# A third of VectorE's exponential shifts, and the attention products with the reciprocal sums, moved to GpSimd; a reordered instruction plan

## The chip, the cores and the metric

The kernel runs on one core of a Trainium2 chip. The core has five engines that run their own instruction streams and meet only at semaphores: TensorE (matrix products, writes PSUM), VectorE and ScalarE (elementwise work, read PSUM and SBUF), GpSimd (elementwise work on SBUF alone) and SyncE, which here issues nearly all DMAs. In the profile they are PE (weight loads apart as PEld), DVE, ACT, POOL and SP. The metric is the device time of one execution in microseconds (us).

## The reference

Two independent blocks on 2048 rows of 512 columns, in bfloat16, written side by side.

```python
# A: 32 query heads of 16, one shared key/value head
q = (x @ wq) -> 32 heads; k = x @ wk; v = x @ wv
p = softmax(q k^T / 4);  a = concat(p v) @ wo
# B: linear attention, 32 heads of 16
pq, pk = q w_phi, k w_phi                  # per head, 16 x 16
phi = concat(softmax(p), softmax(-p))      # 32 features
o = phi_q (phi_k^T v) / (phi_q . sum(phi_k) + 1e-6);  b = o @ wo
out = concat(a, b, axis=-1)
```

Block A needs 32 x 2048 x 2048 exponentials. They are nearly all of the elementwise work.

## The kernel before, in words

**Tiles of block A.** The 2048 x 2048 scores of 32 heads are cut into 32 *accumulations* (`sc`, each with four heads at 512 queries, 16 key blocks of 128). One accumulation has 16 quads, a quad has four score tiles of 128 keys x 512 queries, one per head, 2048 tiles in all. A score tile is one matmul with 32 rows (`score`, L1611); four tiles sit on the four row groups of TensorE. The weighted sums of a quad are added into one PSUM bank (`ACC`) by matmuls with 32 output columns, again four side by side.

**Two ways to an exponential.** Each quad goes one of two ways.

- ScalarE: `expo` (L1672) reads three or two tiles from PSUM banks 0 to 2 or 3 to 4, and writes exp into the ring `PT` (20 tiles). `pv` (L1726) sums a quad with four matmuls.
- VectorE: `next_dq` takes one free bank per tile. `bits` (L1782) turns scores into the bit pattern of an fp16 power of two, as int16: one multiplication and one addition, PSUM to SBUF, `Z[:, 0]`. Then three `shift`s (L1795) add 256, 512 and 768 to all four tiles' 2048 integers, a quarter of an octave each, into `Z[:, 1]` to `Z[:, 3]`. `d_pv` (L1828) sums the four versions, with values weighted by four constants `K`, in 16 matmuls: a weighted mean of four coarse exponentials. There are three such buffers (`NQ`).

In the last accumulation both ways also sum the denominators into a second bank.

**After an accumulation.** `finish_sc` copies the bank to `accS` (L1426) and gathers the row of sums by four DMAs; `finish_sc2` takes the reciprocal of it (L1860) and spreads it by eight more DMAs into `denS`; `finish_sc3` multiplies `accS` by `denS` (L1878, all 31 on VectorE) into `On`. `outproj` (L1897) and `outproj2` project and store it, in 12 blocks. The last accumulation is finished by `out_part` (L1917) and `finish_last`.

**Block B** (`jobs_b`) runs in between: its projections on TensorE, its exponentials on ScalarE (L2050, L2140), its sums, reciprocals and scalings on VectorE.

**What sets the order.** Python code writes out the whole order before the kernel is built. `plan` makes jobs, each with an engine, an assumed duration, its predecessors and a priority; `run` simulates the engines and repeatedly issues the job that can start first, the lower priority number first among those within 0.02 us of it (`rank`). `dq_ok` lets the next VectorE tile start while VectorE's outstanding work (`dbusy`) is at most 3 us. So how many quads go to VectorE is an outcome of the planned times. On the chip each engine runs its stream in that order, with semaphores for the data. Where the plan leaves TensorE idle or lightly used it adds dummy matmuls with zero weights (`put_fill`, `fill` L1420; `company` L1403). The planner's DMA latencies are constants in the calls of `dmas`.

GpSimd has only setup work in the first 22 us, and one small job of block B (`b_kvfin`, L2118).

Of the kernel before, what the change touches and what calls it, by code (L numbers as in the profile page):

```python
# [1169 lines left out]
class _Fast:  # L1170
# [16 lines left out]
    def __init__(self, nc, st, ins, out):  # L1187
# [33 lines left out]
        self.ones = sb("ones", [128, 128], BF)  # L1221
        self.zero = sb("zero", [128, 128], BF)
# [40 lines left out]
        self.last_full = 0.0  # L1263

# [16 lines left out]
    def dmas(self, fs, reads, writes, us, is_output=False):  # L1281

        if self.rec is not None:
            return
        self.S.batch_begin("sp", is_output)
        for f in fs:
            self.S.dma(f, reads=reads, writes=writes)
        self.S.batch_end()
        for r in reads:
            self.tr[r] = max(self.tr.get(r, (0.0, "sp")), (self.fin + us, "sp"))  # L1290
        for w in writes:
            self.tw[w] = (self.fin + us, "sp")
# [37 lines left out]
    def issue(self, j, start):  # L1330
# [11 lines left out]
        self.te[j.eng] = max(self.te[j.eng], start + dur)  # L1342
        self.fin = start + dur + self.TAIL[j.eng]
# [90 lines left out]
    def head(self):  # L1434
# [47 lines left out]
        add("pool", lambda g: g.memset(self.bmx, 0.0), writes=["bmx"])  # L1482
        mask = self.mask
# [15 lines left out]
        for k, t in (("wk_rep", 4.5), ("half1", 3.0), ("wv", 5.5), (("wq", 0), 5.0), (("wq", 1), 16.0), (("VA1", 0), 5.0), (("VA1", 1), 12.0), ("odd", 14.0), ("ones", 1.0), ("zero", 1.0), ("bmx", 8.0)):  # L1499
            self.tw[k] = (t, "sp")  # L1500
# [10 lines left out]
    def jobs_a(self):  # L1511
        ps, xT, job = self.ps, self.xT, self.job
        for kc in range(4):
# [5 lines left out]
            job(("aK", kc), "dve", 0.60, (lambda kc: (lambda: self.absmax(self.KR[:, 0, kc * 512:kc * 512 + 512], kc, [("KR", 0, kc)])))(kc), after=[("KR", 0, kc)], prio=6, rel=30.0 + 5 * kc)  # L1519
# [3 lines left out]
        for ch in range(16):  # L1523
# [4 lines left out]
            job(("aq", ch), "dve", 0.60, (lambda ch: (lambda: self.absmax(self.QA[:, ch % 3, :], 4 + ch, [("QA", ch % 3)])))(ch), after=[("qa", ch)], prio=6, rel=0.0 if ch else 30.0)  # L1528
# [3 lines left out]
        for i in range(4):  # L1532
            job(("pp", i), "pe", 0.87, (lambda i: (lambda: self.out_part(i)))(i), mode="full", nb=1, prio=2.0, ok=lambda: self.ended,
                after=[("on", 24 + a) for a in range(7)])
        for sc in range(31):
            job(("rc", sc), "dve", 0.16, (lambda sc: (lambda: self.finish_sc2(sc)))(sc), after=[("ac", sc)], prio=1.1)
            job(("on", sc), "dve", 0.60, (lambda sc: (lambda: self.finish_sc3(sc)))(sc), prio=1.3,
# [20 lines left out]
    def absmax(self, src, col, reads):  # L1558
        self.add("dve", lambda v: v.tensor_reduce(out=self.mq[:, col:col + 1], in_=src, axis=AX.X, op=ALU.max, apply_absolute_value=True),
                 reads=reads, writes=[("mq", col)])  # L1560
# [107 lines left out]
    def expo(self, n0, us, b0):  # L1668
# [5 lines left out]
        if self.rec is None:  # L1674
# [3 lines left out]
            for n in range(n0, n0 + size):  # L1678
                if n % 4 == 3:
                    q = n // 4  # L1680
                    self.job(("pv", q), "pe", 0.44 if self.aquads[q][0] == 31 else 0.22, (lambda q: (lambda: self.pv(q)))(q), mode="col", prio=1.5,
                             after=[("vb" if self.aquads[q][0] % 2 else "va", self.aquads[q][1] // 4)] + ([("pv", q - 1)] if q else []),
                             ok=(lambda sc: (lambda: self.acc_ok(sc)))(self.aquads[q][0]))
# [29 lines left out]
    def pv(self, q):  # L1713
# [8 lines left out]
        for bank, w, (start, stop) in todo:  # L1722
# [22 lines left out]
    def next_dq(self):  # L1745
# [33 lines left out]
        def bits():  # L1779
# [4 lines left out]
            if self.rec is None:  # L1784
                self.dz_out -= 1
                self.dbusy += 1.2 if h == 3 else -0.6
# [6 lines left out]
        def shift(t):  # L1793
            def go():
                self.add("dve", lambda v: v.tensor_scalar(out=Z[:, t], in0=Z[:, 0], scalar1=256.0 * t, scalar2=None, op0=ALU.add),  # L1795
                         reads=zk, writes=[("Zt", p, t)])
                if self.rec is None:
                    self.dbusy -= 0.6
            return go
        for t in range(1, 4):  # L1800
            self.job(("dS", quad, t), "dve", 0.60, shift(t), after=[("dz", k - x) for x in range(4)], prio=2)
        aft = [("dS", quad, t) for t in range(1, 4)]
# [5 lines left out]
    def d_pv(self, quad):  # L1808
# [7 lines left out]
        rd += [("Z", p, h) for h in range(4)] + [("Zt", p, t) for t in range(1, 4)]  # L1816
# [17 lines left out]
    def d_pd(self, quad):  # L1834
# [4 lines left out]
        rd = ["onesK"] + [("Z", p, h) for h in range(4)] + [("Zt", p, t) for t in range(1, 4)]  # L1839
        self.d_sums(self.den_bank, self.onesK, self.Z[:, p].bitcast(F16), sl, start, stop, rd)  # L1840

    def finish_sc(self, sc):
# [10 lines left out]
        self.dmas(fs, [("accS", r)], [("denC", r)], 4.4)  # L1853
# [3 lines left out]
    def finish_sc2(self, sc):  # L1857
# [8 lines left out]
        self.dmas(fs, [("denR", r)], [("row", r), ("denS", r)], 4.4)  # L1866
# [5 lines left out]
        self.dmas(fs, [("row", r)], [("denS", r)], 11.0)  # L1872

    def finish_sc3(self, sc):
# [3 lines left out]
        self.add("dve", lambda v: v.tensor_tensor(out=o, in0=accS[:, r, :], in1=R[:, r, :], op=ALU.mult),  # L1878
                 reads=[("accS", r), ("denS", r), ("row", r)], writes=[key])
        if r:  # L1880
# [4 lines left out]
            self.dmas(fs, [key], [("On", sl)], 5.0)  # L1885
# [15 lines left out]
    def outproj2(self, qt):  # L1901
# [5 lines left out]
        self.dmas([lambda q: q.dma_start(dst, oa[:, ring, :])], [("outA", ring)], [], 4.0, is_output=True)  # L1907


    def out_part(self, i):  # L1910
        ps, On = self.ps, self.On
        bank = self.bank(("pp", i))

        def fn(pe):
            mm = None
            for A in range(4):
                mm = pe.matmul(ps[:, bank, :], lhsT=On[:, A, i * 128:i * 128 + 128], rhs=self.wo2[:, A, :], start=(A == 0), stop=False)  # L1917
            return mm
        self.add("pe", fn, reads=[("On", A) for A in range(4)] + ["wo2"], writes=[("PS", bank)])

    def finish_last(self):
# [8 lines left out]
        for h in range(2):  # L1930
# [3 lines left out]
            for i in range(2 * h, 2 * h + 2):  # L1934
                bank = self.bank(("pp", i))
# [494 lines left out]
```

## Time and profile before

| | us |
|---|---|
| median of 3 runs | 769.65 (767.93 to 771.23) |
| the profiled execution's own time | 767.89 |
| its span, first to last instruction | 765.8 |
| PE / DVE / ACT / POOL busy | 716.3 / 712.0 / 742.8 / 18.5 |

TensorE's granted clock was 0.995 on average. *Busy* is the union of an engine's instructions; a group's *mean* is one instruction from start to end, and neighbours on VectorE overlap by some 0.08 us. *Idle before* tells how long the engine had stood still before the instructions of the group, and the line after the arrow what ended that. A DMA queue's row is an issue, with the time to landing.

### The profile page before, as it was taken

What the parts mean: (1) busy time and instruction counts of PE and PEld (TensorE: products, weight loads), DVE (VectorE), ACT (ScalarE), POOL (GpSimd) and SP (SyncE); (2) the same over time, 40 slices, a digit from 0 to 9 for tenths busy, and PEclk for the clock granted to TensorE, in tenths of its full rate; (3) what the DMA queues carried; (4) which work ended last, traced back from release to release, by engine and by line L of the source; (5) the groups of instructions that cost most, each with busy time, mean ns of one, the idle gap of its engine ahead of it and who ended that gap; (6) DMA issues with size and microseconds to landing.
All of it is one profiled execution on the core that took longest, in us unless ns stands there. A gap on an engine that the chain in (4) does not pass through costs nothing.

```text
span 765.8 us, 17760 instructions
## 1 busy us (share of the span) xinstructions
PE 716.3 (94%) x7536; PEld 240.5 (31%) x7596; DVE 712.0 (93%) x1242; ACT 742.8 (97%) x694; POOL 18.5 (2%) x73
## 2 busy tenths in 40 slices
PE   7999999999998999999999999999999999999997
PEld 3332333233332333333332332223333333333222
DVE  3999999999998998799999999999997999999991
ACT  5999999999999999999999999999998999999996
POOL 6000000000000002000000000000000000000000
PEclk9999999999999999999999999999998999999999
DMA  9911011111012101110111110112111011111102
GB/s 183 206 9 8 6 8 13 8 10 12 1 12 36 9 6 8 13 9 16 19 9 19 16 15 14 15 11 30 22 20 8 20 28 25 23 15 12 10 8 38
DMA packets 47521, 18.15 MB, mean 24 GB/s; under 512 B 38468, under 2 KB 45572, under 8 KB 47432
## 3 DMA queue, kind: packets, MB, share of 16 engines
q1 hardware_dynamic: 44920, 16.47, 16.6%
q8 instruction: 61, 1.00, 0.5%
q10 hardware_dynamic: 2512, 0.44, 0.4%
q14 instruction: 28, 0.23, 0.1%
HBM read 2.15 MB, written 4.19 MB: 8 GB/s over the span
## 4 chain that ended last, share of the span: by engine, by line
ACT 73%; DVE 12%; PE 11%; DMA 2%; SPq 1%; issue 0%; ACTq 0%
ACT f_PT L1672 70%; DVE f_Z L1782 4%; PE f_ps L1611 3%; DVE f_Z L1795 3%; PE f_ps L1828 2%; ACT f_ET L2140 2%; PE f_ps L1726 2%; ACT f_Ek L2050 1%; DVE f_ssum L2056 1%; DMA f_AxT<-in_A_x_dram 1%; DVE f_vS L2082 1%; DVE f_Wk L2196 1%; PE f_ps L1420 1%; PE f_ps L1403 0%; PE f_ps L1917 0%
## 5 line engine op out<-in xcount | busy, mean ns | idle before, releaser
L1672 ACT ACTIVATE f_PT<-f_ps 128x1536 bf16<-128x1536 f32 x623 | 716.3, 1311 | 14.9 <-DVE f_VK L1581 8.2
L1782 DVE TENSOR_SCALAR f_Z<-f_ps 128x512 int16<-128x512 f32 x492 | 320.7, 680 | 17.4 <-PE f_ps L1611 15.8
L1611 PE MATMUL f_ps<-f_QA,f_KR 32*128 32x512 bf16 x2048 | 314.7, 385 | 23.2 <-ACT f_PT L1672 11.2
L1795 DVE TENSOR_SCALAR f_Z<-f_Z 128x2048 int16<-128x2048 int16 x369 | 243.0, 684 | 0.4
L1611 PEld LDWEIGHTS f_ps<-f_QA,f_KR 32*128 32x128 bf16 x2048 | 81.7, 91 | 237.7 <-ACT f_PT L1672 134.5
L1726 PE MATMUL f_ps<-f_PT,f_VA 128*32 128x512 bf16 x1556 | 153.5, 391 | 2.2 <-DVE f_accS L1426 1.8
L1828 PE MATMUL f_ps<-f_Z,f_VK 128*32 128x512 f16 x1968 | 129.5, 383 | 1.1 <-DVE f_accS L1426 0.4
L1726 PEld LDWEIGHTS f_ps<-f_PT,f_VA 128*32 128x32 bf16 x1556 | 38.7, 93 | 98.9 <-issue 88.3
L1420 PE MATMUL f_ps<-f_ones,f_zero 128*128 128x512 bf16 (+10 forms) x372 | 66.2, 345 | 3.0 <-POOL f_zero L1438 1.3
L1828 PEld LDWEIGHTS f_ps<-f_Z,f_VK 128*32 128x32 bf16 x1968 | 42.4, 96 | 56.9 <-issue 12.6
L1403 PE MATMUL f_ps<-f_ones,f_zero 32*128 32x512 bf16 x144 | 49.4, 380 | 0.3
L1420 PEld LDWEIGHTS f_ps<-f_ones,f_zero 128*32 128x32 bf16 (+2 forms) x372 | 19.1, 97 | 32.7 <-issue 21.9
L2196 DVE TENSOR_TENSOR f_Wk<-f_ps,f_wq 128x512 bf16<-128x512 f32 x32 | 21.8, 683 | 0.0
L1426 DVE COPY f_accS<-f_ps 128x512 f32<-128x512 f32 x31 | 21.3, 686 | 0.1
L2140 ACT ACTIVATE f_ET<-f_ps 128x512 bf16<-128x512 f32 x32 | 20.1, 772 | 0.0
L2082 DVE TENSOR_TENSOR f_vS<-f_ps,f_rs 128x1024 bf16<-128x1024 f32 x16 | 19.5, 1219 | 0.0
L2056 DVE TENSOR_REDUCE f_ssum<-f_Ek 128x64 f32<-128x1024 bf16 x16 | 19.3, 1208 | 0.1
L2050 ACT ACTIVATE f_Ek<-f_ps 128x512 bf16<-128x512 f32 x32 | 19.3, 721 | 0.0
L2072 PE MATMUL f_ps<-f_Bwv,f_BxT 128*128 128x512 bf16 x53 | 14.3, 380 | 2.8 <-DVE f_outA L1426 1.2
L2133 PE MATMUL f_ps<-f_BxT,f_Wq 128*128 128x512 bf16 x54 | 14.5, 380 | 2.0 <-issue 1.2
L2042 PE MATMUL f_ps<-f_Wk,f_BxT 128*128 128x512 bf16 x57 | 15.0, 381 | 1.4 <-issue 0.6
L1403 PEld LDWEIGHTS f_ps<-f_ones,f_zero 32*128 32x128 bf16 x144 | 11.4, 92 | 15.1 <-issue 11.4
(100 smaller groups left out, 320.6 us busy)
## 6 DMA issues: line engine op xcount, KB each, us to landing
f_denS<-f_denS SPq DMA_DIRECT2D x124, 30.0 KB, 3.1
out_dram<-f_outB SPq DMA_DIRECT2D x16, 128.0 KB, 2.7
f_denC<-f_accS SPq DMA_DIRECT2D x124, 2.0 KB, 1.7
f_denS<-f_denC SPq DMA_DIRECT2D x124, 2.0 KB, 1.7
out_dram<-f_outA SPq DMA_DIRECT2D x14, 128.0 KB, 2.1
f_On<-f_Od SPq DMA_DIRECT2D x60, 16.0 KB, 1.8
f_Bwv<-in_B_wqkv_dram SPq DMA_DIRECT2D x1, 512.0 KB, 4.7
f_Bwo<-in_B_wo_dram SPq DMA_DIRECT2D x1, 512.0 KB, 5.3
```

Of the source, the lines that this page charges most:

```text
L1403: self.add("pe", lambda pe: pe.matmul(out, lhsT=zero[0:32, :], rhs=rhs, start=False, stop=False, tile_position=(0, 0)), reads=["ones", "ze ...
L1420: mm = pe.matmul(ps[x:x + m, bank, 0:n].rearrange("p (a n) -> p a n", n=128), lhsT=zero[0:r, 0:m], rhs=rhs, start=start, stop=start, **kw)
L1611: return pe.matmul(self.ps[:, bank, :], lhsT=self.KR[32 * g:32 * g + 32, sc % 2, kap * 128:(kap + 1) * 128], rhs=self.QA[32 * g:32 * g + 3 ...
L1672: self.add("act", lambda a: a.activation(out=PT[:, sl[0]:sl[0] + size, :], in_=ps[:, b0:b0 + size, :], func=ACT.Exp), reads=[("PS", b0 + i ...
L1726: mm = pe.matmul(ps[32 * g:32 * g + 32, bank, :], lhsT=w, rhs=PT[:, slots[g], :], start=start, stop=stop, tile_position=(0, 32 * g))
L1782: self.add("dve", lambda v: v.tensor_scalar(out=o, in0=ps[:, bank, :], scalar1=self.Z1, scalar2=self.Z0, op0=ALU.mult, op1=ALU.add), reads ...
L1795: self.add("dve", lambda v: v.tensor_scalar(out=Z[:, t], in0=Z[:, 0], scalar1=256.0 * t, scalar2=None, op0=ALU.add), reads=zk, writes=[("Z ...
L1828: mm = pe.matmul(ps[32 * g:32 * g + 32, bank, :], lhsT=w[:, k, :], rhs=Zf[:, k, sl[g], :], start=start and k == 0, stop=stop and k == 3, t ...
L2050: self.add("act", (lambda a, sg: (lambda e: e.activation(out=Ek[:, r, a].rearrange("p h f -> p (h f)"), in_=ps[:, bank, :], func=ACT.Exp, ...
L2082: self.add("dve", lambda v: v.tensor_tensor(out=vS[:, :, :, 0:16], in0=v3, in1=rs.unsqueeze(3).to_broadcast([128, 2, 32, 16]), op=ALU.mult ...
L2140: self.add("act", lambda e: e.activation(out=self.ET[:, sl, :], in_=self.ps[:, bank, :], func=ACT.Exp, scale=sg), reads=[("PS", bank)], wr ...
L2196: self.add("dve", lambda v: v.tensor_tensor(out=o, in0=i, in1=w.unsqueeze(3).to_broadcast([128, 16, 2, 16]), op=ALU.mult), reads=[("PS", b ...
```

## The change

1. `shift` takes an engine. VectorE makes the versions 1 and 2 as before. Version 3 is made on GpSimd: the four tiles' 2048 16-bit integers are read as 1024 32-bit integers, and 768 x 65537, which is 768 in both halves, is added from a one-element tile that is broadcast (`step3`). It reads both VectorE versions as dependencies too, so it starts after VectorE's two shifts of that quad. `PSH = 4` of four tiles go this way.
2. `finish_sc3` runs on GpSimd for the first 28 (`ONP`) of the 31 products.
3. The planner takes shifts and products (`PAIR`) on VectorE and all GpSimd jobs as excluding each other (`port`): one side's job does not start before the other side's last one ends. This is in the plan only; no semaphore stands for it.
4. The planner's DMA latencies are smaller, and it models SP's queue (`spq`, 0.64 us per issue).
5. `rank` adds a pseudo-random offset of up to half a unit to each priority, with a seed for each 20 us of the plan (`SEEDS`); the window of 0.02 us becomes 0.06 or 0.12 for some seeds.
6. At the end: `out_part` is cut into single matmuls that may be issued earlier; the denominators of `pv` come before its sums; all four last outputs are issued on SP's queue, two of which ScalarE issued before. Dummies may also go to an `ACC` bank that is not open.

`AENG`, `SENG` and `PVN` are set so that nothing changes by them.

```diff
-        def shift(t):
+        def shift(eng, t, a, b):
             def go():
-                self.add("dve", lambda v: v.tensor_scalar(out=Z[:, t], in0=Z[:, 0], scalar1=256.0 * t, scalar2=None, op0=ALU.add),
-                         reads=zk, writes=[("Zt", p, t)])
+                if eng == "pool":
+                    w = lambda x: Z[:, x, a:b].bitcast(I32).rearrange("p a n -> p (a n)")
+                    self.add("pool", lambda g: g.tensor_tensor(out=w(t), in0=w(0), in1=self.step3.to_broadcast([128, 256 * (b - a)]), op=ALU.add),
+                             reads=zk + ["step3"] + [("Zt", p, x, "dve") for x in (1, 2)], writes=[("Zt", p, t, eng)])
+                    return
+                self.add(eng, lambda v: v.tensor_scalar(out=Z[:, t, a:b], in0=Z[:, 0, a:b], scalar1=256.0 * t, scalar2=None, op0=ALU.add),
+                         reads=zk, writes=[("Zt", p, t, eng)])
...
         for t in range(1, 4):
-            self.job(("dS", quad, t), "dve", 0.60, shift(t), after=[("dz", k - x) for x in range(4)], prio=2)
-        aft = [("dS", quad, t) for t in range(1, 4)]
+            n = 4 - self.PSH if t == 3 else 4
+            if n:
+                aft.append(("dS", quad, t))
+                self.job(aft[-1], "dve", 0.07 + 0.133 * n, shift("dve", t, 0, n), after=[("dz", k - x) for x in range(4)], prio=2)
+            if n < 4:
+                self.job(("dP", quad), "pool", self.PDUR, shift("pool", t, n, 4), after=list(aft), prio=2)
+                aft.append(("dP", quad))
...
-        self.add("dve", lambda v: v.tensor_tensor(out=o, in0=accS[:, r, :], in1=R[:, r, :], op=ALU.mult),
+        self.add("pool" if sc < self.ONP else "dve", lambda v: v.tensor_tensor(out=o, in0=accS[:, r, :], in1=R[:, r, :], op=ALU.mult),
...
+                    if r is not None and (j.name[0] in self.PAIR or j.eng == "pool"):
+                        r = max(r, self.port["dve" if eng == "pool" else "pool"])
...
-                now = [o for o in opts if o[0] <= lo + 0.02]
+                seed = self.seed(lo)
+                now = [o for o in opts if o[0] <= lo + (0.02, 0.02, 0.06, 0.12)[seed % 4]]
...
+        if seed:
+            p += self.JITTER * (zlib.crc32(("%d%s" % (seed, j.name)).encode()) / 4294967296.0 - 0.5)
...
+    AENG, ADUR, SENG, SDUR, ONP, ODUR = 'dve', 0.6, 'dve', 1.13, 28, 1.35
+    PSH = 4
+    PDUR = 2.15
+    PAIR = ("dS", "on", "dP")
```

113 lines of the change are left out of this document (72 added, 41 removed).

## The prediction

> **What bounds the kernel now.** I read the page from the top (busy time, then the chain that ended last), then cut the span into head, middle and tail, then the groups and the waits of VectorE.
>
> ```profile
> span 765.8 us, 17760 instructions
> ...
> PE 716.3 (94%) x7536; PEld 240.5 (31%) x7596; DVE 712.0 (93%) x1242; ACT 742.8 (97%) x694; POOL 18.5 (2%) x73
> ...
> ACT 73%; DVE 12%; PE 11%; DMA 2%; SPq 1%; issue 0%; ACTq 0%
> ```
>
> Three engines look full, GpSimd (POOL) is idle. The chain of waits lies on ScalarE for 73%. The stretches (PE, weight load, DVE, ACT, POOL busy, with instruction counts) tell where each is full:
>
> ```profile
> core 0: us, PE busy (x) PEld busy (x) DVE busy (x) ACT busy (x) POOL busy (x), PEclk, DMA share, GB/s
> 0.00:10.30 10.30, 7.16 (x41) 2.78 (x41) 2.64 (x7) 1.28 (x1) 7.24 (x32) 1.00 0.98 171
> 10.30:753.00 742.70, 701.51 (x7438) 235.12 (x7500) 707.09 (x1232) 736.03 (x685) 11.27 (x41) 1.00 0.16 21
> 753.00:765.80 12.80, 7.66 (x66) 2.64 (x59) 2.26 (x4) 5.51 (x10) 0.00 (x0) 1.00 0.14 45
> ```
>
> The head (10.3 us, until the first exponential) and the tail (12.8 us) are not touched by who does the exponentials. In the middle, 742.7 us, ScalarE works 736.0 us: it is the bound, with 6.7 us idle. VectorE works 707.1 us and is idle for 35.6. The two share one pool of 2048 score tiles; whichever gets time free takes more. So the middle ends where the two balance, and TensorE decides only if its real work fills it.
>
> ```profile
> L1672 ACT ACTIVATE f_PT<-f_ps 128x1536 bf16<-128x1536 f32 x623 | 716.3, 1311 | 14.9 <-DVE f_VK L1581 8.2
> L1782 DVE TENSOR_SCALAR f_Z<-f_ps 128x512 int16<-128x512 f32 x492 | 320.7, 680 | 17.4 <-PE f_ps L1611 15.8
> L1795 DVE TENSOR_SCALAR f_Z<-f_Z 128x2048 int16<-128x2048 int16 x369 | 243.0, 684 | 0.4
> L1726 PE MATMUL f_ps<-f_PT,f_VA 128*32 128x512 bf16 x1556 | 153.5, 391 | 2.2 <-DVE f_accS L1426 1.8
> L1828 PE MATMUL f_ps<-f_Z,f_VK 128*32 128x512 f16 x1968 | 129.5, 383 | 1.1 <-DVE f_accS L1426 0.4
> L1420 PE MATMUL f_ps<-f_ones,f_zero 128*128 128x512 bf16 (+10 forms) x372 | 66.2, 345 | 3.0 <-POOL f_zero L1438 1.3
> L1403 PE MATMUL f_ps<-f_ones,f_zero 32*128 32x512 bf16 x144 | 49.4, 380 | 0.3
> ```
>
> 492 conversions and 369 shifts are 123 VectorE groups of 4 tiles; ScalarE does the other 1556 tiles.
>
> **The prices.** A piece of the chain in order of time (start, us, what), and VectorE's timeline (start, us, engine, line):
>
> ```profile
> 326.22 68.05 ACT f_PT L1672 x60
> ```
>
> ```profile
> 76.64 1.88 DVE L1782 TENSOR_SCALAR f_Z<-f_ps 128x512 int16<-128x512 f32 x3
> ```
>
> ```profile
> 505.23 0.69 DVE L1878 TENSOR_TENSOR f_Od<-f_accS,f_denS 128x512 bf16<-128x512 f32 x1
> 505.83 1.29 DVE L1795 TENSOR_SCALAR f_Z<-f_Z 128x2048 int16<-128x2048 int16 x2
> ```
>
> Sixty exponentials of 3 and 2 tiles in turn are 150 tiles in 68.05 us: 0.4537 us a tile, 1.815 us for a group of 4. On VectorE a conversion, a shift and a product each hold the engine 0.60 us: (1.88 - 0.68)/2 from three in a row, 1.29 - 0.69 from two, 505.83 - 505.23 for the product. The 0.68 to 0.69 of one overlaps the next.
>
> **The change, part by part.** *The third shift leaves VectorE.* 123 x 0.60 = 73.8 us of its time goes; a group costs it 6 x 0.60 = 3.6 us in place of 4.2.
>
> *Products with the reciprocal sums.* The first 28 of 31 go to GpSimd: 28 x 0.60 = 16.8 us.
>
> *Refill.* VectorE's work for 123 groups falls to 707.1 - 73.8 - 16.8 = 616.5 us; with its idle time as it is, 652.1. ScalarE's stretch is 742.7. Each further group adds 3.6 there and takes 1.815 here, so they meet after (742.7 - 652.1)/(3.6 + 1.815) = 16.7 further groups, at 742.7 - 16.7 x 1.815 = 712.4 us. The same division gives the price of an idle microsecond on VectorE: 1.815/5.415 = 0.335 us of the span.
>
> *The addition on GpSimd* has no row: 1024 32-bit elements, two inputs, one of them one element repeated. The nearest rows, groups by shape:
>
> ```profile
> L2118 POOL TENSOR_TENSOR f_KVn<-f_kvS,f_mask 128x128 bf16<-128x128 f32 x8 | 3.6, 448 | 276.7 <-DVE f_kvS L2109 276.2
> L2123 POOL TENSOR_TENSOR f_KVs<-f_kvS,f_mask 128x64 bf16<-128x64 f32 x1 | 0.3, 318 | 0.1
> L1476 POOL MEMSET f_denS<- 128x1024 f32 x1 | 1.0, 955 | 0.1
> ```
>
> and one line's durations (min/median/max), with the two engines' timelines at that place:
>
> ```profile
> L2118 POOL TENSOR_TENSOR f_KVn<-f_kvS,f_mask x8: 399/402/773, 298.2 to 302.0; 128x128 bf16<-128x128 f32 x8
> ```
>
> ```profile
> 298.25 1.73 POOL L2118 TENSOR_TENSOR f_KVn<-f_kvS,f_mask 128x128 bf16<-128x128 f32 x3 [276.18 <-DVE f_kvS L2109]
> ```
>
> ```profile
> 298.08 0.68 DVE L1795 TENSOR_SCALAR f_Z<-f_Z 128x2048 int16<-128x2048 int16 x1
> 298.68 0.68 DVE L1559 TENSOR_REDUCE f_mq<-f_QA 128x1 f32<-128x512 bf16 x1
> 299.27 0.68 DVE L1782 TENSOR_SCALAR f_Z<-f_ps 128x512 int16<-128x512 f32 x1
> ```
>
> The line through 402 ns at 128 and 318 at 64 elements rises 1.31 ns an element and gives 318 + 960 x 1.31 = 1.58 us; in proportion to 402 it is 8 x 402 = 3.2 us; the write-only memset of that size, 0.96 us, bounds it below. I take 2.2, near the middle of the two two-input bounds (the diff plans with 2.15, an assumption). A product of 512 elements is 0.9 by the line, 1.6 in proportion; I take 1.25. [...]
>
> At 140 groups GpSimd is busy 140 x 2.2 + 28 x 1.25 = 343 us of 712, 48%. Hidden, as long as it does not hold up VectorE. On that the trace has one case: the eight additions of L2118 last 402 ns, but the one that began at 298.25, inside a shift begun at 298.08, lasted 773 and so ended about 0.4 us after that shift's 0.60 us were over. A GpSimd instruction with SBUF inputs stood still until the shift had gone. The reduction behind the shift, with one SBUF input, ran beside GpSimd in its usual 0.68 us and gave way to a conversion after 0.59: it held nobody and was not held. That a shift stands still behind GpSimd is not shown; I count it as possible. [...]
>
> Between a group's second shift and the next group's first lie four conversions from PSUM, 4 x 0.60 = 2.4 us, against 2.2 of GpSimd: the natural order keeps them apart, and the new planner does not start a shift while it believes GpSimd busy, nor the reverse. What it does not keep apart are VectorE's other instructions on SBUF alone. Those with one input I cost at nothing, by the reduction at 298.68; no row shows one with two inputs beside GpSimd, so these count:
>
> ```profile
> L2062 DVE TENSOR_TENSOR f_bmx<-f_ssum,f_bmx 128x64 f32<-128x64 f32 x16 | 3.5, 219 | 0.0
> L2174 DVE TENSOR_TENSOR f_wq<-f_wq,f_rden 128x256 f32<-128x256 f32 x4 | 1.6, 408 | 0.0
> L2170 DVE TENSOR_TENSOR f_rden<-f_sden 128x128 f32<-128x128 f32 x4 | 1.1, 282 | 0.0
> ```
>
> 24 of them, in 48% of the cases beside GpSimd, half an addition (1.1 us) each: 12.7 us, times 0.335: +4.2 us. Bounds: nothing, and 24 x 2.2 x 0.335 = 17.7; I take the mean case, since nothing shows which engine would give way.
>
> *Who waits for the new wait.* The addition waits for two shifts; behind it on GpSimd's queue stand products and the next additions, and for it waits TensorE's product of the group. A buffer of Z is then held for a period of 712.4/139.7 = 5.1 us of conversions, 1.2 of shifts, 2.2 of GpSimd and 16 x 129.5/1968 = 1.05 of matmuls, 9.6 us; with three buffers a group may take 15.3. The third buffer hides it. A product on GpSimd waits for a chain of DMAs:
>
> ```profile
> f_denS<-f_denS SPq DMA_DIRECT2D x124, 30.0 KB, 3.1
> f_denC<-f_accS SPq DMA_DIRECT2D x124, 2.0 KB, 1.7
> ```
>
> ```profile
> 735.01 0.69 DVE L1426 COPY f_accS<-f_ps 128x512 f32<-128x512 f32 x1
> ```
>
> ```profile
> 750.81 0.69 DVE L1878 TENSOR_TENSOR f_On<-f_accS,f_denS 128x512 bf16<-128x512 f32 x1 [4.48 <-DMA f_denS<-f_denS]
> ```
>
> From copy to product 15.8 us, and the copy's buffer is needed again two accumulations later, about 2 x 742.7/32 = 46 us: hidden. The planner's latencies come down to about these figures (4.0 for the 3.1, 1.8 for the 1.7, after 0.64 per issue on SP). If a product gets to the queue's head before its data, the addition behind it is late too; the 5.7 us spare of Z cover one such wait. SP's queue gains two output transfers at the end, which ScalarE issued before, and nothing in the middle.
>
> *TensorE.* A group moved adds 1.05 us of products less 4 x 153.5/1556 = 0.39: 16.7 x 0.66 = 11 us. Its 701.5 hold 66.2 + 49.4 of dummy products (L1420, L1403) that the planner only puts into gaps or where activity is low; real work is about 586 + 11 = 597 of 712. It has room if the dummies give way.
>
> *Searched order.* Random shifts of the priorities, one seed per 20 us. It can only remove idle time; VectorE's longest waits:
>
> ```profile
> DVE f_Z L1782 <- PE f_ps L1611: 15.8, 20, 2.9
> DVE f_On L1878 <- DMA f_denS<-f_denS: 4.5, 1, 4.5
> DVE f_outA L1426 <- DMA out_dram<-f_outA: 3.6, 1, 3.6
> ```
>
> 24 us. All of it would be 8 us of the span; an order that fits the chip worse than the present one could lose as much. As most of it is many short waits for TensorE, which the dummies that give way can shorten, I take -3.
>
> *Tail.* Twelve matmuls of the output projection, which stood behind the last accumulation, may go into earlier gaps, and the denominators are summed first.
>
> ```profile
> 757.19 2.76 PE L1917 MATMUL f_ps<-f_wo,f_On 128*128 128x512 bf16 x12
> 758.89 0.48 DVE L1932 SCALAR_TENSOR_TENSOR f_Od<-f_ps,f_odd,f_ET 128x256 bf16<-128x256 f32 x1 [0.24 <-ACT f_ET L1928]
> ```
>
> They end at 759.95; the work that they precede could not be complete before VectorE's 758.89 + 0.48 = 759.37. Gain at most 0.6; all four outputs on SP's queue may take it back: -0.5, between -1 and +1. The pooled constant (one small memset) and the copies of planner times cost nothing visible.
>
> **The sum.** 10.3 + 712.4 + 12.8 = 735.5; -0.5 tail, +4.2 collisions, -3 order: 736.2 us of span. The profiled execution took 767.89, 2.1 above its span, and the median of the three runs shown is 1.8 above that: 740.
>
> **Rivals.** *GpSimd slower than planned.* At 3.2 us an addition outlasts the four conversions, by about 1 us over what the order was written for. If half of 139 groups pay it at the next shift: 70 us idle, x 0.335 = 23: 763. For it: the 402 ns at 128 elements; against: the rise of only 1.31 ns an element.
>
> *The lock, the other way round* (slower). If VectorE's order brings a shift soon after the previous group's second one, that shift and all behind it stand still for the rest of the addition. The point that decides: 90.6 us over 123 groups, 0.74 us a group; beyond it nothing is gained. At half an addition, 1.1 us a group, the balance is 652.1 + 135.3 + 4.7 d = 742.7 - 1.815 d, d = -6.9, a middle of 755.2 and 782 in all. For it: the 0.4 us stall at 298.25, and that VectorE's order already mixes (the rows at 505.23 have a product and two shifts in a row, not a group's three). Against: the planner holds both apart.
>
> *Freed time is not filled.* Conversions wait for TensorE (15.8 us already) with two free banks; if VectorE only idles more, by the full 90.6 us, the balance stays where it was: 768 to 770. Against: 115.6 us of dummies can go.
>
> *The order wins more*: all 24 us of waits and no collisions, 735.5 - 0.5 - 8 + 3.9 = 731, and lower, to 725, where ScalarE's 6.7 us of idle go too.
>
> **How the numbers follow.** Forecast (728 to 752): 0.64; GpSimd slower (752 to 764): 0.13; lock: 0.13; not filled: 0.04; order wins more than that (below 727): 0.06. The range 727 to 764 leaves out the lock and the last, 0.19, and most of the not-filled case. A measurement of this kernel tells about 0.5%, 3.8 us: faster 0.64 + 0.13 + 0.06 = 0.83, same 0.04, slower 0.13.
>
> **What would show it.** Conversions up from 492 to about 560, shifts from 369 to about 280 (two per group), GpSimd additions about 140 of some 2.2 us; ScalarE still near 99% of the middle, its exponential group down by 30 us. Shifts well over 0.69 us, or conversions waiting after a shift, would be the lock; idle VectorE time put down to TensorE would be the unfilled case. The forecast falls if VectorE's idle time in the middle passes about 125 us.

## The result, and the profile after

The changed kernel takes 774.42 us (median of 20 runs, 770.25 to 779.65) against 767.96 (765.59 to 773.59) for the kernel before, measured side by side: a ratio of 1.0075, 95% interval 1.0055 to 1.0094. It is slower by 0.75% where 740 was forecast. The profiled execution took 774.72 us; its mean granted TensorE clock was 0.982 (0.995 before).

The page of the changed kernel, in the order in which the prediction read the one before: busy time, then the chain that ended last.

```profile
span 773.0 us, 18117 instructions
...
PE 725.3 (94%) x7646; PEld 238.1 (31%) x7646; DVE 682.7 (88%) x1133; ACT 733.5 (95%) x682; POOL 307.9 (40%) x232
...
ACT 51%; PE 23%; DVE 23%; DMA 1%; issue 1%; SPq 0%; DVEq 0%
```

ScalarE held 73% of the chain and holds 51% now; TensorE and VectorE have 23% each. The stretches, with the same columns as in the prediction:

```profile
0.00:10.30 10.30, 7.86 (x43) 3.03 (x44) 3.03 (x9) 1.88 (x2) 7.34 (x33) 1.00 0.95 175
10.30:760.00 749.70, 709.12 (x7548) 232.80 (x7549) 677.45 (x1120) 725.29 (x672) 300.53 (x199) 0.98 0.16 21
760.00:773.00 13.00, 8.27 (x65) 2.22 (x57) 2.25 (x4) 6.34 (x10) 0.00 (x0) 1.00 0.15 47
```

Head and tail are as long as before. The middle was to shrink from 742.7 to 712.4 us and grew to 749.7. In it ScalarE stands idle for 749.7 - 725.3 = 24.4 us (6.7 before) and VectorE for 72.3 (35.6 before). The groups (busy, mean ns of one, idle before):

```profile
L1683 ACT ACTIVATE f_PT<-f_ps 128x1536 bf16<-128x1536 f32 (+1 forms) x611 | 703.6, 1293 | 31.4 <-PE f_ps L1622 22.2
L1813 POOL TENSOR_TENSOR f_Z<-f_Z,f_step 128x1024 int32<-128x1024 int32 x130 | 251.9, 1938 | 423.8 <-DVE f_Z L1816 422.8
L1798 DVE TENSOR_SCALAR f_Z<-f_ps 128x512 int16<-128x512 f32 x520 | 337.9, 680 | 45.5 <-PE f_ps L1622 32.5
L1816 DVE TENSOR_SCALAR f_Z<-f_Z 128x2048 int16<-128x2048 int16 x260 | 187.3, 740 | 1.6 <-PE f_ps L1855 0.7
```

The change does what it says: two shifts per VectorE group, the third an addition on GpSimd. But there are 520 conversions, 130 groups: 7 more than before, where 16.7 were forecast. And the mean shift takes 740 ns, 684 before. The longest waits that matter (us in total, times, longest):

```profile
DVE f_Z L1798 <- PE f_ps L1622: 32.5, 53, 2.3
ACT f_PT L1683 <- PE f_ps L1622: 22.2, 35, 2.1
```

VectorE's wait for score tiles was 15.8 us; ScalarE's was 5.9, eleven times.

**Who is late.** Durations of one line's instructions (ns, min/median/max), first the shifts and the casts of the kernel before, then the changed kernel:

```profile
L1795 DVE TENSOR_SCALAR f_Z<-f_Z x369: 628/685/724, 24.2 to 745.6; 128x2048 int16<-128x2048 int16 x185
L1426 DVE CAST f_vS<-f_rs x16: 298/307/324, 84.4 to 292.4; 128x64 bf16<-128x64 f32 x16
```

```profile
L1816 DVE TENSOR_SCALAR f_Z<-f_Z x260: 624/682/2383, 22.2 to 752.9; 128x2048 int16<-128x2048 int16 x130
L1813 POOL TENSOR_TENSOR f_Z<-f_Z,f_step x130: 1890/1892/2274, 24.8 to 753.6; 128x1024 int32<-128x1024 int32 x130
L2091 DVE TENSOR_TENSOR f_bmx<-f_ssum,f_bmx x16: 197/224/1578, 70.0 to 281.4; 128x64 f32<-128x64 f32 x16
L1434 DVE CAST f_vS<-f_rs x16: 292/310/1105, 78.3 to 291.2; 128x64 bf16<-128x64 f32 x16
```

Medians are as before; the maxima are not. Summed over all instructions of VectorE, what one lasted beyond its group's median (from 60 ns up, nothing before) is 24.6 us: 15.4 in 16 shifts, 5.1 in 7 of the 16 two-input maxima, 3.6 in 5 of the 16 casts of the reciprocals, 0.5 in one other. I call this the *excess*. Two places on the timeline (start, us), first a shift:

```profile
108.61 3.58 DVE L1816 TENSOR_SCALAR f_Z<-f_Z 128x2048 int16<-128x2048 int16 x3
109.37 2.27 POOL L1813 TENSOR_TENSOR f_Z<-f_Z,f_step 128x1024 int32<-128x1024 int32 x1 [3.82 <-DVE f_Z L1816]
```

Three shifts in a row, 1.88 us by their price, take 3.58. The first completes a group, and GpSimd's addition starts at 109.37, just after the second shift, which belongs to the next group, has begun. The addition ends 0.38 us late (2.27 for 1.89): it waited for the second shift. The third shift, due at 109.8, ends at 112.19, 0.55 us after the addition: it waited for GpSimd. In the written order the addition came after that third shift (the third experiment makes it wait for that); here it starts once its own two shifts are done. Then a shift behind a product with the reciprocal sums:

```profile
125.74 1.27 POOL L1905 TENSOR_TENSOR f_Od<-f_accS,f_denS 128x512 bf16<-128x512 f32 x1
126.05 1.51 DVE L1816 TENSOR_SCALAR f_Z<-f_Z 128x2048 int16<-128x2048 int16 x1
```

It ends at 127.56, 0.55 us after the product's 127.01. A product starts when its DMAs land, wherever VectorE then is: of the 15.4 us that GpSimd stood idle before its products, at least 12.7 ended with a DMA into `denS`. Of the 16 late shifts 11 stood behind a product (7.5 us in all), 4 were such thirds in a row (6.8 us), and one stood behind an addition. In the prediction's row of 773 ns GpSimd's instruction stood behind a shift, as the addition does here by 0.38 us; in both places a shift stands behind GpSimd, by 1.70 us (3.58 for 1.88) and by 0.83 (1.51 for 0.68). This is what I call the *lock*.

**What follows from a late instruction.** A little further in the same stretch:

```profile
112.27 1.89 POOL L1813 TENSOR_TENSOR f_Z<-f_Z,f_step 128x1024 int32<-128x1024 int32 x1 [0.63 <-DVE f_Z L1816]
113.35 0.89 DVE L2091 TENSOR_TENSOR f_bmx<-f_ssum,f_bmx 128x64 f32<-128x64 f32 x1
...
115.31 0.39 PE L1622 MATMUL f_ps<-f_QA,f_KR 32*128 32x512 bf16 x4 [2.18 <-DVE f_Z L1798]
...
115.78 3.71 ACT L1683 ACTIVATE f_PT<-f_ps 128x1536 bf16<-128x1536 f32 x3 [1.57 <-PE f_ps L1622]
```

The maximum, 0.22 us alone, stands until the addition ends (114.16). The conversions behind it free their banks late, TensorE waits 2.18 us for a bank, and ScalarE, the bound, 1.57 us for score tiles that stand behind in TensorE's queue. The same place in the first experiment below, where the order is the same and GpSimd's work is cut to nothing:

```profile
110.11 1.89 DVE L1820 TENSOR_SCALAR f_Z<-f_Z 128x2048 int16<-128x2048 int16 x3
113.17 0.22 DVE L2096 TENSOR_TENSOR f_bmx<-f_ssum,f_bmx 128x64 f32<-128x64 f32 x1
...
113.52 6.11 ACT L1687 ACTIVATE f_PT<-f_ps 128x1536 bf16<-128x1536 f32 x5
```

The three shifts take their price, the maximum its 0.22 us, and ScalarE goes on without a wait.

**The clock.** There are also stretches in which the granted clock is below 1. One lies a little later in the trace (the last figures: clock, DMA share, GB/s):

```profile
120.00:130.00 10.00, 9.50 (x133) 3.66 (x130) 9.89 (x17) 9.86 (x9) 3.16 (x2) 1.00 0.24 19
130.00:140.00 10.00, 9.63 (x79) 2.62 (x76) 9.23 (x15) 7.88 (x8) 3.78 (x2) 0.83 0.02 3
```

```profile
130.62 1.19 PE L1622 MATMUL f_ps<-f_QA,f_KR 32*128 32x512 bf16 x3
132.29 1.89 PE L1612 MATMUL f_ps<-f_AxT,f_wq 128*128 128x512 bf16 x4
```

Four full matmuls take 1.89 us there; elsewhere in this trace four of that shape take 1.04. ScalarE works 7.88 of these 10 us. Eight windows of 10 us have a clock of 0.93 or less, one before. Across the 20 runs the time goes with it: 768.5 us of span at a clock of 0.989, 777.9 at 0.968. A straight line through them, 4.6 us for each 0.01 of clock, reaches 767 us of span at the 0.995 of the kernel before, whose span is 766. By this estimate the loss against the kernel before goes with the clock, and the 34 us that are missing against the forecast do not; whether the clock is low because of the waits is not shown. In the stretch with the longer durations, 130.62 to 134.10, the clock is 0.58; in the 3.6 us before it the clock was 1.00 and TensorE busy for 2.92. What brings a lapse is not shown. The first experiment below, whose excess is 0.2 us, has lapses as well: four windows of 10 us at 0.93 or less, 0.66 at the lowest.

### The profile page after: what moved, and what is told of

Same layout as the page of the kernel before. It is cut to its first block, busy times and chain, and to the rows that moved or that the text cites. A ratio compares the mean times of both kernels' runs of the same rounds, so it can differ in the third digit from the quotient of the medians.

```text
span 773.0 us, 18117 instructions
## 1 busy us (share of the span) xinstructions
PE 725.3 (94%) x7646; PEld 238.1 (31%) x7646; DVE 682.7 (88%) x1133; ACT 733.5 (95%) x682; POOL 307.9 (40%) x232
## 3 DMA queue, kind: packets, MB, share of 16 engines
q1 hardware_dynamic: 45208, 16.74, 16.6%
## 4 chain that ended last, share of the span: by engine, by line
ACT 51%; PE 23%; DVE 23%; DMA 1%; issue 1%; SPq 0%; DVEq 0%
ACT f_PT L1683 48%; DVE f_Z L1798 9%; PE f_ps L1622 8%; DVE f_Z L1816 6%; PE f_ps L1855 5%; PE f_ps L1742 4%; ACT f_ET L2169 2%; DVE f_ssum L2085 1%; PE f_ps L1428 1%; DVE f_vS L2111 1%; PE f_ps L1411 1%; PE f_ps L1612 1%; PE f_ps L1924 1%; DVE f_accS L1434 1%; ACT f_Ek L2079 1%; DVE f_bmx L2091 1%
## 5 line engine op out<-in xcount | busy, mean ns | idle before, releaser
L1683 ACT ACTIVATE f_PT<-f_ps 128x1536 bf16<-128x1536 f32 (+1 forms) x611 | 703.6, 1293 | 31.4 <-PE f_ps L1622 22.2
L1813 POOL TENSOR_TENSOR f_Z<-f_Z,f_step 128x1024 int32<-128x1024 int32 x130 | 251.9, 1938 | 423.8 <-DVE f_Z L1816 422.8
L1798 DVE TENSOR_SCALAR f_Z<-f_ps 128x512 int16<-128x512 f32 x520 | 337.9, 680 | 45.5 <-PE f_ps L1622 32.5
L1816 DVE TENSOR_SCALAR f_Z<-f_Z 128x2048 int16<-128x2048 int16 x260 | 187.3, 740 | 1.6 <-PE f_ps L1855 0.7
L1742 PE MATMUL f_ps<-f_PT,f_VA 128*32 128x512 bf16 x1528 | 149.1, 392 | 0.8 <-DVE f_accS L1434 0.4
L1855 PE MATMUL f_ps<-f_Z,f_VK 128*32 128x512 f16 x2080 | 138.2, 386 | 0.5 <-PE f_ps L1742 0.5
L1742 PEld LDWEIGHTS f_ps<-f_PT,f_VA 128*32 128x32 bf16 x1528 | 37.3, 93 | 92.2 <-issue 82.5
L1428 PE MATMUL f_ps<-f_ones,f_zero 128*32 128x512 bf16 (+11 forms) x345 | 60.7, 360 | 1.5 <-POOL f_zero L1446 1.3
L1428 PEld LDWEIGHTS f_ps<-f_ones,f_zero 128*32 128x32 bf16 (+2 forms) x345 | 17.7, 99 | 23.8 <-issue 18.0
L1905 POOL TENSOR_TENSOR f_On<-f_accS,f_denS 128x512 bf16<-128x512 f32 x14 | 19.0, 1357 | 10.8 <-DMA f_denS<-f_denS 9.8
L1905 POOL TENSOR_TENSOR f_Od<-f_accS,f_denS 128x512 bf16<-128x512 f32 x14 | 18.3, 1308 | 4.6 <-DMA f_denS<-f_denS 2.9
L1612 PE MATMUL f_ps<-f_AxT,f_wq 128*128 128x512 bf16 x64 | 17.4, 397 | 0.5 <-DVE f_Z L1798 0.5
```

Of the source, the lines that this page charges most:

```text
L1428: mm = pe.matmul(ps[x:x + m, bank, 0:n].rearrange("p (a n) -> p a n", n=128), lhsT=zero[0:r, 0:m], rhs=rhs, start=start, stop=start, **kw)
L1683: self.add("act", lambda a: a.activation(out=PT[:, sl[0]:sl[0] + size, :], in_=ps[:, b0:b0 + size, :], func=ACT.Exp), reads=[("PS", b0 + i ...
L1742: mm = pe.matmul(ps[32 * g:32 * g + 32, bank, :], lhsT=w, rhs=PT[:, slots[g], :], start=start, stop=stop, tile_position=(0, 32 * g))
L1798: self.add("dve", lambda v: v.tensor_scalar(out=o, in0=ps[:, bank, :], scalar1=self.Z1, scalar2=self.Z0, op0=ALU.mult, op1=ALU.add), reads ...
L1813: self.add("pool", lambda g: g.tensor_tensor(out=w(t), in0=w(0), in1=self.step3.to_broadcast([128, 256 * (b - a)]), op=ALU.add), reads=zk ...
L1816: self.add(eng, lambda v: v.tensor_scalar(out=Z[:, t, a:b], in0=Z[:, 0, a:b], scalar1=256.0 * t, scalar2=None, op0=ALU.add), reads=zk, wri ...
```

## The experiments

Theory A is the lock: VectorE's instructions on SBUF stand behind GpSimd's, and that costs the gain. Its rivals, by letter in the expectations, are that the order is slow by itself and the lock costs little (B), that the searched order is what costs time (C), and that the planner's other changes do (D). One more, without a letter, is GpSimd's latency: the third version is ready later. For the groups that did not move there are two theories: three buffers stop the refill (E), or TensorE is full (F). "Before" was 767.9 to 768.6 us throughout. Ratios are to it, with 95% intervals.

**GpSimd's work cut to nothing, order unchanged.**

```diff
-  in0=w(0), in1=self.step3.to_broadcast([128, 256 * (b - a)]), op=ALU.add
+  (the same, with out, in0 and in1 cut to [:, 0:2]; a product on GpSimd likewise to [:, 0:2])
```

> The changed kernel in the same order and with the same waits, but GpSimd's additions and its 28 products work on 2 elements each, so that GpSimd is busy for a fraction; the third versions and these products are left out of the result. Theory A (VectorE stands still behind GpSimd, TensorE and ScalarE follow): the 7 further groups take their 7 x 1.815 = 12.7 us, so about 755, between 750 and 760, no shift over 0.76 us, ScalarE's waits for TensorE back from 22 us to 6 to 10. Theory B (the order itself is slow, TensorE is full, the lock costs little): 769 to 776.

Measured: 758.16 us, 0.986 (0.981 to 0.9909); excess 0.2 us; ScalarE's waits for score tiles 8.8 us. Of these 3.1 are one wait near the start, behind memsets that this kernel needs. So the durations on GpSimd, not order, waits or plan, cost 16.3 us of the 774.4 (give or take some 4, by the interval). They act by holds or by latency; the kernels further on, which have the latency without most of the holds, tell these apart. At the prediction's 0.335 us for each microsecond lost on VectorE the excess of 24.6 would cost 8.2; ScalarE's waits, 22.2 us with the holds, are the nearest thing to the other half; that they make it up is argued. The clock is no more than a part of it: it is 0.987 here in the profiled execution.

**Only the products cut.** Same edit for L1905 alone.

> The changed kernel in the same order; GpSimd's additions are whole, and only its 28 products work on 2 elements each (these products are left out of the result). It splits the 16 us of the lock. If the products, behind which 11 of the 16 late shifts stood, cost the most: 760 to 766. If the additions do, which also hold the two-input instructions: 767 to 773.

Measured: 769.6 us, 1.0012 (0.998 to 1.0044); excess 15.4. The products cost about 5 us, the additions the other 11, each give or take 3 to 5.

**The plan's exclusion made real for additions.**

```diff
+  hold = [self.last_shift]          # the last shift issued before this addition
-  reads=zk + ["step3"] + [("Zt", p, x, "dve") for x in (1, 2)]
+  reads=zk + ["step3"] + [("Zt", p, x, "dve") for x in (1, 2)] + hold
```

> The changed kernel in the same order, and each GpSimd addition waits also for the last shift that VectorE was given before it in the written order, so that it cannot start between two shifts that the plan puts in front of it. Theory A: the late shifts that follow two shifts (4 of 16, up to 1.7 us each) go, 769 to 773. Theory B: no change, 773 to 776, or slower by the later additions.

Measured: 765.67 us, 0.997 (0.9946 to 0.9993). A gain of 8.8, more than expected. No shift is late as the third in a row any more; 12 of the 13 late ones are behind products, and the excess is still 17.8. From the end of its group's second shift to its own end an addition takes 2.30 us on average here and 2.19 in the changed kernel: GpSimd's latency is no shorter, so it does not explain the gain. GpSimd takes the added wait: it is busy for 302.6 of 768.6 us.

**Without the search.** `SEEDS` all zero.

> The changed kernel without the seeds, so in the planner's own order. Theory A: 128 groups, and as many collisions, 773 to 783. Theory C (the searched order is fragile and costs the time): faster than the changed kernel, 760 to 768.

Measured: 778.17 us, 1.0118 (1.0076 to 1.0161); excess 23.8, clock 0.972. The order without search is slower, not faster: C falls. The search may be worth some 4 us; the two intervals overlap.

**Without search, and the plan blind to the exclusion** (`PAIR = ()`).

> The changed kernel without seeds and with a plan that does not know that VectorE's shifts and GpSimd exclude each other; 129 groups. Theory A: more and longer late shifts than in the one with that knowledge (24 us), 778 to 790. Theory B: within 1% of it either way, 772 to 786.

Measured: 794.64 us, 1.0363 (1.0291 to 1.0436); excess 36.1, of which 31.0 in 41 late shifts. That is more than theory A expected. The exclusion in the plan, though nothing enforces it, is worth 16 us.

**The new planner with nothing on GpSimd.** `PSH = 0`, `ONP = 0`, no seeds.

> The new planner without the seeds and with nothing on GpSimd (all shifts and products on VectorE): what the planner's latencies, the new dummies and the tail do alone. Theory A: 123 groups and the time of the kernel before, 764 to 771. Theory D (the planner changes cost the time): 773 or more.

Measured: 765.85 us, 0.9971 (0.9944 to 0.9998); 123 groups as before, no excess. The shorter latencies, SP's queue in the plan and the changes at the end cost nothing.

**The exclusion completed.** The plan also keeps the maxima with the reciprocals, the casts and the small products of block B (`qw`) apart from GpSimd, and additions and products really wait for the last shift, maximum or cast written before them; `PDUR` 2.0, `ODUR` 1.4, own search.

```diff
-  PAIR = ("dS", "on", "dP")
+  PAIR = ("dS", "on", "dP", "rs", "vs", "qw")
```

> The changed kernel with a plan that also keeps VectorE's other users of SBUF alone (the maximum with two inputs, the cast of the reciprocals, the small products of block B) apart from GpSimd, with real waits: each GpSimd addition and product waits also for the last such instruction that VectorE was given before it; its own searched order, 130 groups. Theory A (the lock is what costs): VectorE's late instructions fall from 24.6 us below 10, 755 to 762, and clearly under the 765.7 of the kernel that held only shifts apart. Theory B (the order): 764 to 772.

Measured: 758.85 us, 0.987 (0.9827 to 0.9914); excess 8.0, all of it in shifts. Then the same with all 31 products on VectorE (`ONP = 0`), with search and without:

> The same, but all 31 products with the reciprocal sums stay on VectorE, so GpSimd has only additions, whose start the written order knows better than that of products that wait for DMAs; 128 groups. Theory A: no shift late behind a product, 755 to 762, in spite of two groups less (3.6 us). If the products' 16.8 us of VectorE time are what the change gains, it is slower than the kernel with products on GpSimd by 4 us or more.

> The kernel with all products on VectorE, the wider plan and the real waits, without the search for an order: 128 groups as with it. If the placing of GpSimd's work is what gains, 754 to 760, little behind the 754.7 with the search; if the search gains it, 762 or more.

Measured: **754.72 us, 0.983 (0.9806 to 0.9854)**, and without search 761.6, 0.9921 (0.9899 to 0.9943). Giving VectorE back 28 products, 16.8 us of its time, does not cost the 4 us or more that a gain from the products would have been worth; the 4 us that it seems to gain lie within overlapping intervals, and each of the two kernels has a searched order of its own. Without search the result lies between the two forecasts: against the same without the waits and with products on GpSimd (778.17) the placing gains 16.6 us, and the search another 6.9. GpSimd's latency, from the second shift's end to the addition's, is 2.25 us on average with search and 2.13 without, against 2.19 in the changed kernel and 2.04 in that without search: it stays and the time goes, so the holds cost the time and not the latency. The middle of the kernel with search, and the durations of its shifts and additions:

```profile
10.30:740.00 729.70, 700.75 (x7538) 233.06 (x7535) 662.98 (x1136) 727.13 (x678) 253.79 (x170) 1.00 0.17 22
```

```profile
L1817 DVE TENSOR_SCALAR f_Z<-f_Z x256: 628/686/1412, 26.1 to 729.3; 128x2048 int16<-128x2048 int16 x128
L1814 POOL TENSOR_TENSOR f_Z<-f_Z,f_step x128: 1890/1892/1893, 29.2 to 730.1; 128x1024 int32<-128x1024 int32 x128
```

ScalarE works 727.1 of 729.7 us again, the additions are never held, the excess is 4.1 us.

**Why only 7 groups moved.** In the next kernels GpSimd's work is cut to nothing, the products are on VectorE and the exclusion is off, so that neither GpSimd nor the lock limits. TensorE reads the second version twice in place of the third. First three `Z` buffers, then four, both without search:

```diff
-  rhs=Zf[:, k, sl[g], :]
+  rhs=Zf[:, min(k, 2), sl[g], :]    # the third version isn't kept
-  NQ = 3
+  NQ = 4                            # second kernel only
```

> No seeds, all products on VectorE, and GpSimd's addition works on 2 elements in a scratch tile; the third version is left out, and TensorE's products use the second in its place, so that a buffer of Z has three versions; three buffers. VectorE then has two shifts a group and no lock. 128 groups by the written order. Theory E (three buffers stop the refill) and theory F (TensorE is full) both expect 755 to 762 and VectorE idle for over 70 us.

> The kernel with three buffers and no lock, but with four buffers of Z in the memory that the third versions took; 135 groups by the written order. Theory E: the 7 further groups take 7 x 1.815 = 12.7 us, 743 to 749, ScalarE still over 98% of the middle. Theory F: TensorE cannot carry more, ScalarE waits for it, 753 or more.

Measured: 768.08 us (0.9986, 0.9955 to 1.0018) with three, 782.78 (1.0215, 1.0184 to 1.0245) with four. Both theories expected 755 to 762 with three buffers, and both missed. The likely reason, not shown, is the order: the kernel above, also with 128 groups and no search, takes 761.6 with whole additions. Four buffers take 135 groups, and the last exponential ends at 740.1 us in place of 750.7, 10.6 us earlier, where seven groups of 1.815 would make it 12.7. But then 39.7 us of other work are left, in which ScalarE does almost nothing:

```profile
739.90:779.60 39.70, 23.74 (x208) 11.16 (x200) 21.40 (x44) 2.91 (x7) 0.00 (x0) 0.85 0.13 40
```

```profile
ACT f_outB L1972 <- PE f_ps L1963: 27.5, 2, 27.2
```

It is mostly block B's projections and sums, which the plan put off behind block A's further groups. ScalarE's last copies wait 27.2 us for it. The same with four buffers in an order searched for the earliest end:

> The kernel with four buffers and no lock, in a searched order in which the work of block B is done in time; 130 groups by the written order. Theory E (buffers alone stop the refill): under 748. Theory F (TensorE is full once the buffers give way): 750 to 756, no better than the 754.7 with three buffers and GpSimd's whole additions.

Measured: 753.88 us, 0.9817 (0.9797 to 0.9836), with 130 groups. The search gives five of the groups back and is worth 28.9 us here. This is the best order found for additions that cost nothing, with all products on VectorE, and the kernel with real additions (754.72) is within 0.9 us of it. Last, a quarter of TensorE's work per VectorE group is left out, with four buffers and with three, again without search:

```diff
-  for k in range(4):
+  for k in range(3):                # 12 matmuls for a VectorE quad, 16 before
-  self.job(("dpv", quad), "pe", 0.87, ...)
+  self.job(("dpv", quad), "pe", 0.65, ...)
```

> As the kernel with four buffers and without search (e8_four_buffers: GpSimd's addition on two elements, no third version in Z), but the third version's four matmuls are left out of every VectorE quad as well, so that TensorE makes 12 in place of 16 matmuls for it; the plan is told 0.65 us in place of 0.87. Nothing else is taken away: buffers, free banks, VectorE's and ScalarE's instructions are as there. Theory F (once the buffers give way TensorE's own work and its free time decide how much can move): the plan has 134 VectorE groups (135 there), so the balance of VectorE and ScalarE is the same and the last exponential may stay near 739 us; but the 27 us of block B's projections that were left for the end fit in between, and the kernel ends at about 750 us in all (744 to 756) against 782.8. If TensorE was not the limit, and block B came late because VectorE or the banks had no room for it, it ends again 20 us or more after the last exponential, at 770 to 783.

> The same with three buffers, to be set beside e7_three_buffers (768.1, 128 groups, last exponential near 750, 14 us of late work at the end). The plan has 131 groups. Theory F: with less work for TensorE the late work goes and three further groups move, 5 us of exponentials: about 752 (748 to 758). If the three buffers alone held the number of groups at 128, or TensorE's work were not what came late, it stays at 764 to 770. It should stay above the same with four buffers by 2 to 6 us, three groups of 1.8 us.

Measured: 750.84 us (0.9777, 0.9728 to 0.9825) with four buffers, 756.31 (0.9872, 0.9822 to 0.9922) with three: 32 and 12 us less than the same with 16 matmuls, and both as theory F expected. With four buffers, the stretch up to 737 us and the end:

```profile
0.00:737.00 737.00, 700.98 (x7222) 229.09 (x7222) 680.95 (x1181) 720.58 (x670) 49.47 (x208) 1.00 0.18 24
737.00:750.40 13.40, 5.04 (x29) 1.37 (x25) 2.26 (x4) 3.19 (x7) 0.00 (x0) 0.80 0.15 45
```

134 groups, the last exponential at 737.6, and a tail of 13 us: the late work is gone. So TensorE's work per group matters, as F has it: with less of it block B's work is done in time. With 16 matmuls TensorE had spent at least 89.0 us on dummies (44.0 + 30.0 + 15.0 in its three largest groups of them) and had still left that work behind: in that order their time was not used as room. Two limits of this: the number of groups itself goes with the buffers (128 to 135, and 131 to 134), not with TensorE's work (134 for 135, 131 for 128). And every one of these kernels has an order of its own: the search took 28.9 us out with 16 matmuls, and an order without search with 12 lies only 3.0 us below that. How much a matmul less is worth apart from the order is not shown. What fills TensorE beyond the matmuls' own time is argued, not tested. A piece of TensorE's timeline of the kernel before:

```profile
345.16 0.40 PE L1726 MATMUL f_ps<-f_PT,f_VA 128*32 128x512 bf16 x4
345.49 0.39 PE L1611 MATMUL f_ps<-f_QA,f_KR 32*128 32x512 bf16 x2
345.81 0.40 PE L1726 MATMUL f_ps<-f_PT,f_VA 128*32 128x512 bf16 x4
346.14 0.62 PE L2210 MATMUL f_ps<-f_ident,f_Wk 128*128 128x128 bf16 x8
```

From one shape of matmul (32 columns, 32 rows, full) to the next the starts lie 0.32 to 0.33 us apart; in a row of full matmuls, 1.04 us for four of 0.39, they lie 0.22 apart. About 0.1 us for each of 1,287 changes of shape would be, as an estimate, some 129 us of TensorE's 716 busy ones.

## Why the prediction was wrong, step by step

Put into the prediction's balance, the middle of 749.7 us comes out with five terms that it did not have. VectorE's idle time in the middle is up by 36.7 us, its excess is 24.6, and another 11.1 of its busy time I can't assign to any group (as an estimate, 104 x 0.08 = 8.3 us of it is overlap of neighbours that is lost: 189 of its instructions start after a gap there, 85 before); at 0.335 these are 12.3 + 8.2 + 3.7 us. ScalarE has 17.7 us more idle time and 2.0 more work than its tiles by price; at 3.6/5.415 = 0.665 these are 11.8 + 1.3. Together 37.3, which is 749.7 - 712.4. The terms add up by construction and name no cause by themselves; the steps below do.

- **"Refill": failed.** 16.7 further groups were to move, 7 did. The step let nothing but VectorE's and ScalarE's time decide. With the lock mostly or wholly out of the way the best orders found moved 5 and 7 as well (754.72 and 753.88 us), and gained 13 to 14 us; these keep the products on VectorE, for which the same division gives 73.8/5.415 = 13.6 groups. So with 16 matmuls a group no order found had more than about half of the 30 us that the middle was to lose.
- **"TensorE has room if the dummies give way": failed, and with it the refill.** I took 49.4 us of L1403 and 66.2 of L1420 off its 701.5 as if they were free time. But 135 groups with 16 matmuls left 39.7 us of work behind the last exponential beside at least 89.0 us of dummies, and 12 in place of 16 took 32 and 12 us off. How much of this is TensorE's time and how much the order in which it is used is not shown. "Freed time is not filled", a rival at 0.04, was half right.
- **"Collisions", +4.2, and "the natural order keeps them apart": failed.** They cost 16.3 us. The step averaged over 24 two-input instructions, of which no row had shown one held; the late ones were first of all 16 shifts, then the maxima as counted, then casts with one input, which the step had at nothing from one reduction. It trusted the plan for shifts, though no semaphore stands for the exclusion, and it let products start where the plan had them. It also priced a held microsecond as VectorE's time alone, 0.335, which makes 8.2; with what follows behind, on TensorE and ScalarE, it came to twice that.
- **The lock as a rival (slower, 0.13): its mechanism came**, smaller than its price: 24.6 us in all, 0.19 us a group, where it put the point of no gain at 0.74. It needed no more because half of the gain was missing already.
- **The stated sign, "falls if VectorE's idle time passes about 125 us": wrong.** Idle time and excess reached 97 and the forecast had fallen; the sign left out ScalarE's own idle time.
- **Durations: right.** An addition takes 1.89 us (2.2 taken, bounds 0.96 to 3.2), so GpSimd was not slower than planned; a product 1.27 (1.25 taken). GpSimd is busy for 308 us (343 forecast for 140 groups).
- **SP's queue, latencies, tail: right.** The planner's other changes cost nothing (765.85 us with nothing on GpSimd). "The third buffer hides it" was half right: a fourth lets the plan move 7 groups more (135 for 128), but the best order with four is no faster than with three (753.88 and 754.72). The -3 us for the searched order was of the right size by the 4 us in this kernel and 7 in the best, though the 4 are not clear of noise, and with four buffers it was 28.9.

## What to carry to other kernels

The exclusion between VectorE and GpSimd that existed only in the plan was not kept on the chip (24.6 us of excess; 8.0 and 4.1 with real waits): turn such a one into a wait of GpSimd's instruction, put on every kind of VectorE instruction that the trace shows late, and be wary of work on GpSimd whose start hangs on a DMA (11 of the 16 late shifts stood behind such products). Before freed time is turned into a gain, price the next resource per unit moved, here TensorE's matmuls; its dummies and its busy share did not tell how much room it had (at least 89.0 us of dummies beside 39.7 us of late work). Cutting that work in one run tells more, best beside a searched order, as two orders differed by 28.9 us here. In this kernel additions alone, with real waits, give 754.72 us, 1.7% below the kernel before.

## What the runs showed of the hardware that I had not expected

- A VectorE cast with one SBUF input (128 x 64, f32 to bf16) was held by GpSimd as well: 310 ns as the median, 1105 at most. The five of 16 that began inside an addition were all late, while none of the reductions and reciprocals was, though 34 of them ran beside GpSimd for 0.1 us or more.
- Both engines were held within one microsecond: at 109.37 the addition waited 0.38 us for a shift, and the next shift 1.70 us for the addition.
- Holds on VectorE, which is not the bound (1.70 us at 109.81, 0.67 at 113.35), reached ScalarE through PSUM banks (2.18 us of wait on TensorE) and TensorE's queue (1.57 us of wait at 115.78).
- The granted clock differed between kernels that kept TensorE about equally busy: 0.982 in the changed kernel (94%), 0.987 with GpSimd's work cut to nothing in the same order (95%), 0.998 in the kernel with additions alone and real waits, whose order is another and whose TensorE is as busy (95%).
